# Steps 0 and 1 of a gated attention with an FFN behind it: one batch with 256 tokens a unit in place of two batches with 128

## The chip, the core and the metric

The kernel runs on one core of a Trainium2 chip. The metric is the device time of one execution in microseconds (us). The kernel before took 195.69 us, the median of three runs (195.66 to 196.28).

## What is computed

A recurrent attention with a decay for each key channel is followed by a feed-forward network with a ReLU gate. There are 4 batches, 8 heads, 768 tokens and 48 channels a head; the model width is 384 and the hidden width 1536.

```python
f = 1.0 / (1.0 + np.exp(-f_logit))
state = zeros((B, H, D, D)); y = zeros_like(q)
for t in range(S):
    state = f[:, :, t, :, None] * state + einsum('bhd,bhe->bhde', k[:, :, t], v[:, :, t])
    y[:, :, t] = einsum('bhd,bhde->bhe', q[:, :, t], state)
x = y.transpose(0, 2, 1, 3).reshape(B * S, H * D)          # 3072 x 384
out = (maximum(x @ w_gate, 0.0) * (x @ w_val)) @ w_out     # 1536 hidden
```

Inputs and output are float32 in HBM; the matmuls take bfloat16.

## The kernel before, in words

**Tiling.** The 768 tokens are cut into six steps of 128 tokens (`c` = 0 to 5). A step takes the four batches, two by two (pair `pr` = 0, 1). A step's attention gives 4 x 128 columns of `xT` (channels on partitions), and its FFN (`ffn_hidden`, `ffn_out`) works on these 512 columns: 12 blocks `j` of 128 hidden channels, each a gate group and a value group of three matmuls (L834), a ReLU on ACT (L840), a product on DVE (L844), then `w_out` (L877). In steps 0 to 2 the first six blocks run on 256 columns at a time (`halves`), so that a pair's FFN can begin before the other pair is done.

**Attention of a step.** ACT forms exp and log of the gate's logits (`f_in`, then `bneg`). TensorE sums the logs over tokens with a triangle of ones ("cum", L572 and L658). ACT takes exp of the sum with both signs. The products with `k` and `q` are the "hats" (POOL and DVE), which are transposed so that channels lie on partitions (`qkT`). TensorE multiplies them ("scores", L724), DVE masks the scores with a triangle (`ptm`, L734, four instructions a pair), and TensorE multiplies these with `vpad` and the query with the old state ("intra", L759). A product of `k` hats and `vpad` ("state", L810) updates the state on DVE and POOL (L543, L547, L549).

**Variants by step.** Step 0 is the only member of `twos`: a partition holds two neighbouring tokens of one of the pair's two batches, so a load of f, k or q has rows of 384 bytes in place of 192, and `v` is loaded one token a partition. `attention_pair` handles the pair's two batches as one. For the state update, `attention_back` transposes step 0's `k` back (L631) once the step's intra matmuls are done. In steps 1 and 2 (`pe_hats`) TensorE transposes the hats, eight 128x128 transposes a batch (L694), and DVE copies them out of PSUM (L699); in steps 3 to 5 a DMA transpose through the crossbar, issued from SP (L702), does this. In steps 0 to 2 intra is "tiled": 32-column array tiles give `xT`'s layout at once. In steps 3 to 5 it is "natural" (L767, L771), and a crossbar DMA transposes x (L795).

**Order.** A planner (`Plan`) is given every operation with a cost, a priority and the buffers that it touches, and lists each engine's instructions in one fixed order. Engines run in that order and wait on semaphores. Loads are issued from SP in a fixed order (`first`); the weights are issued from POOL. In `first`, `wg0@f0.1` means that weight slice 0 waits until the load of `f`, step 0, pair 1 has landed; `f1.0@wv1` likewise. While TensorE waits at the start, it runs matmuls on zeros (L938).

Of the kernel before, what the change touches and what calls it, by code (L numbers as in the profile page):

```python
# [299 lines left out]
def bass_hgrn2_outer__then__ffn_reglu_kernel(  # L300
# [10 lines left out]
    twos = (0,)  # L311
    pe_hats = {(1, 0), (1, 1), (2, 0), (2, 1)}
    halves = {0: 6, 1: 6, 2: 6}
    x_way = {(c, pr): "tiled" if c < 3 else "xbar" for c in range(6) for pr in range(2)}
    s_twin = {(c, pr) for c in range(6) for pr in range(2)} - {(0, 0), (1, 0)}
    y_twin = {(1, 1), (2, 0), (2, 1)}
# [5 lines left out]
    C = 128  # L322
# [30 lines left out]
    dec = [sb(f"dec{i}", [128, B, NP, 2], F32) for i in range(NA)]  # L353
# [20 lines left out]
    pick2 = sb("pick2", [128, 2], BF16)  # L374
    ident = sb("ident", [128, 128], BF16)
# [4 lines left out]
    pl = Plan({"bc": 2, "bc4": 4, "tp": 2, "s": 4, "y": 2, "kv": 1, "f": 4})  # L380
# [28 lines left out]
    def triangle(t, name, base, prio):  # L409
# [9 lines left out]
                                         pattern=[[0, 64], [1, 2]], channel_multiplier=-1), ["pick"], ["pick"], occ=0.3, prio=-20)  # L419
# [10 lines left out]
    add("DVE", lambda: ve.tensor_copy(pick2[:], same.ap[:, 0:2]), [same], ["pick2"], occ=0.1, prio=-19)  # L430
# [8 lines left out]
    for i in range(NA):  # L439
        fill("DVE", f"dec{i}", dec[i][:], 0.0, 32, -14)  # L440
# [20 lines left out]
    def load(n, c, b0, b1, after=()):  # L461
        last = tails.get("load")
        t = ld[n]
        both = c in twos and n != "v"
        if both:
            src = bass.AP(tensor=srcs[n].tensor, offset=b0 * H * S * D + c * C * D,
                          ap=[[2 * D, C // 2], [S * D, 2 * H], [1, 2 * D]])
            dst = bass.AP(tensor=t, offset=slot_of(n, c, b0 // 2) * 2 * HD, ap=[[NL[n] * 2 * HD, 128], [2 * D, H], [1, 2 * D]])
        else:
            src = bass.AP(tensor=srcs[n].tensor, offset=b0 * H * S * D + c * C * D,  # L470
                          ap=[[D, C], [S * D, (b1 - b0) * H], [1, D]])
            dst = t[:, slot_of(n, c, b0 // 2), :, :, :].rearrange("p b h d -> p (b h) d")
        op = add("SP", lambda: sy.dma_start(dst, src), [], in_keys(n, c, b0, b1),  # L473
                 occ=0.7 if both else 1.0, lat=0.9, prio=c * 100, after=after,
                 follows=[last] if last else [])
        tails["load"] = op
        dma(op, f"{n}{slot_of(n, c, b0 // 2)}", 0.95 * (b1 - b0), (64, 19, 27) if both else (128, 13.5, 23))
        return op
# [20 lines left out]
    loads, done = [], {}  # L499
    for item in first:  # L500
        item, _, behind = item.partition("@")
        gate = [done[behind]] if behind else []
        if item[0] == "w":
            op = load_w(item[:2], int(item[2:]), gate)
        else:
            c, pr = (int(x) for x in item[1:].split("."))
            op = load(item[0], c, 2 * pr, 2 * pr + 2, gate)
        done[item] = op
        if item[0] != "w":
            loads.append(op)  # L510

    def chain(line, *args, **kw):

        last = tails.get(line)
        tails[line] = add(*args, follows=[last] if last else [], **kw)
        return tails[line]
# [10 lines left out]
    def tokens(c, b, x, p, lo=0, hi=128):  # L527
        qi = (c * B + b) % NQ
        if c not in twos:
            return qkT[lo:hi, qi, x, p, :]  # L530
        row, two = NQ * 2 * NP * C, b % 2
        return bass.AP(tensor=qkT, offset=lo * row + (qi - two) * 2 * NP * C + x * 2 * NP * C + p * 2 * C + two,
                       ap=[[row, hi - lo], [2, C]])
# [18 lines left out]
    def attention_pair(c, b0):  # L552
# [3 lines left out]
        raw = {n: ld[n][:, slot_of(n, c, pr), :, :, :].rearrange("p b h d -> p (b h d)") for n in "fkq"}  # L556
        by_i = {n: raw[n].rearrange("p (h i d) -> p i h d", h=H, i=2) for n in "fkq"}
        key = {n: in_keys(n, c, b0, b0 + 2) for n in "fkq"}
        bi, e0, q0, ai = (w0 // 2) % NB, w0 % NE, w0 % NQ, c % NA
# [5 lines left out]
            follows=tails.pop("first q", []), **act_t(2 * HD))  # L565
        heads = lambda b_: b_.ap[:, 0:HD].rearrange("p (h d) -> p h d", h=H)
        for i in range(2):
            bc, ek = Bank("bc4"), Bank("bc4")

            def cum(i=i, bc=bc):  # L570
                for o in range(2):
# [3 lines left out]
            ex = expo[:, e0 + i, 0, :]  # L575
            add("ACT", lambda bc=bc, ek=ek: sc.activation(ek.ap[:, 0:HD], bc.ap[:, 0:HD], AF.Exp, scale=1.0),
                [bc], [ek], prio=P + 2 + i, opens=[ek], **act_t(HD))
            eqk = bc if i else f"expq{e0}_0"
            add("ACT", lambda bc=bc, i=i, ex=ex: sc.activation(bc.ap[:, 0:HD] if i else ex, bc.ap[:, 0:HD], AF.Exp, scale=-1.0),
                [bc], [eqk], prio=P + 2 + i, **act_t(HD))  # L580
            e, hi = ("DVE" if i else "POOL"), his[i]
            hk_op = add("DVE", lambda i=i, hi=hi, ek=ek: ve.tensor_tensor(hats[:, hi, 1, :, 0:D], by_i["k"][:, i], heads(ek), ALU.mult),
                        key["k"] + [ek, f"hats{hi}"], hk_(hi), prio=P + 2 + i, **dve_t(HD))
            add(e, lambda e=e, i=i, hi=hi, bc=bc, ex=ex: engine[e].tensor_tensor(
                hats[:, hi, 0, :, 0:D], by_i["q"][:, i], heads(bc) if i else ex.rearrange("p (h d) -> p h d", h=H), ALU.mult),
                key["q"] + [eqk, f"hats{hi}"], hq_(hi), prio=P + 3 + i, follows=[hk_op] if i else [], **elem_t(e, HD))
# [9 lines left out]
        for j in range(2):  # L596
            lo = 64 * j
            add("ACT", lambda lo=lo, j=j: sc.activation(
                dec[ai][lo:lo + 64, b0:b0 + 2, :, j].rearrange("p b n -> p n b"),
                tot.ap[lo:lo + 64, 0:2 * NP].rearrange("p (n b) -> p n b", n=NP), AF.Exp, scale=-1.0),  # L600
                [tot, f"dec{ai}"], [f"dec{ai}_{b}{j}{hh}" for b in (b0, b0 + 1) for hh in range(2)], prio=P + 10, **act_t(8))
        for x in (1, 0):
            tp = Bank("tp")

            def transposes(x=x, tp=tp):
                t16 = tp.ap[:, :].bitcast(BF16)
                for p in range(NP):
                    for i in range(2):
                        mm = te.transpose(t16[:, 2 * C * p:2 * C * (p + 1)].rearrange("q (r i b) -> q r i b", i=2, b=2)[:, :, i, :],
# [5 lines left out]
            e = "DVE" if x else "ACT"  # L615
            op = add(e, (lambda tp=tp, dst=dst: sc.activation(dst, tp.ap[:, :].bitcast(BF16), AF.Copy)) if e == "ACT"  # L616
# [3 lines left out]
            if not x and b0 == 0:  # L620
                tails["first q"] = [op]

    def attention_back(c, b, behind):
        w = c * B + b
        hi, qi = w % NH, w % NQ
        tp = Bank("tp")

        def transposes():
            t16 = tp.ap[:, :].bitcast(BF16)
            for p in range(NP):  # L630
                mm = te.transpose(t16[:, p * C:(p + 1) * C], tokens(c, b, 1, p), ident[:])  # L631
            return mm
        P = w * 10
        tails["transposes"] = add("PE", transposes, ["ident", f"qkT{qi}_10", f"qkT{qi}_11"], [tp], occ=0.3, lat=PE_L, prio=P + 30,
                                  opens=[tp], follows=[behind, tails["transposes"]])
        add("DVE", lambda: ve.tensor_copy(hats[:, hi, 1, :, :].rearrange("p h d -> p (h d)"), tp.ap[:, :].bitcast(BF16)[:, 0:4 * C]),
            [tp], hk_(hi), prio=P + 31, follows=[behind], **dve_t(256))

    def attention_front(c, b):
# [32 lines left out]
        if c < NC - 1:  # L672
            for j in range(2):
# [9 lines left out]
        add("POOL", lambda: gp.tensor_tensor(hq, qin[:, b % 2, :, :], ex[:, 0, :].rearrange("p (h d) -> p h d", h=H),  # L683
                                             ALU.mult),
            in_keys("q", c, b, b + 1) + [f"expq{ei // 2 * 2}_{ei % 2}", f"hats{hi}"], hq_(hi), prio=P + 2, **pool_t(HD))
# [21 lines left out]
    def attention(c, bs):  # L707
        units = []
        for b in bs:
# [5 lines left out]
                in_keys("v", c, b, b + 1) + [f"vpad{w % NV}"], [f"v_{w % NV}"], prio=w * 10 + (55 if c in twos else 3), **pool_c(HD))  # L715
# [58 lines left out]
        xi, ybank, yop = c % NX, {}, {}  # L774
        tiled = x_way[c, bs[0] // 2] == "tiled"
        for part in ([units] if tiled and (c, bs[0] // 2) in y_twin else [[u] for u in units]):
# [4 lines left out]
            op = chain("intra", "PE", rows, [t for u in part for t in need(u) + ([f"vpad{u[1] % NV}"] if tiled else [])], ys,  # L781
                       occ=(0.34 if c else 0.19) * len(part) + 0.235 if tiled else 0.38, lat=PE_L, prio=part[0][1] * 10 + 7, opens=ys)
            for u, y in zip(part, ys):
                ybank[u[0]], yop[u[0]] = y, op
        for b, w, _ in units:
# [12 lines left out]
            if c in twos:  # L798
                behind.append(yop[b])
                later.append(lambda b=b, w=w: update(c, b, w))  # L800
            elif c < NC - 1:
                update(c, b, w)

    def update(c, b, w):
# [9 lines left out]
        if c in twos:  # L814
            attention_back(c, b, behind[-1])
        chain("state", "PE", state, hk_(hi) + [f"hats{hi}", f"v_{w % NV}"], [kv],
              occ=0.18, lat=PE_L, prio=P + (32 if c in twos else 6), opens=[kv])
        new_state(kv, c, b, w, P + (25 if c in twos else 0))
# [50 lines left out]
    def ffn_out(g, bs, cuts=1):  # L869
# [14 lines left out]
        for b in bs:  # L884
# [4 lines left out]
            at = (b * S + g * C) * DM  # L889
            both = [(bass.AP(tensor=out.tensor, offset=at, ap=[[DM, C], [1, DM]]), osb[oi][:, :])]  # L890
# [4 lines left out]
    groups = {c: [(0, 2, range(0, n)), (2, 4, range(0, n)), (0, 4, range(n, NJ))] for c, n in halves.items()}  # L895
    pend = []
    for c in range(NC):
# [4 lines left out]
        behind, later = [], []  # L902
        for b in range(0, B, 2):
# [5 lines left out]
            attention(c, (b, b + 1))  # L909
        for rest in later:  # L910
            rest()
# [22 lines left out]
    order = pl.settle([(bk, warm_until if bk is spare else 0.0) for bk in banks], rounds=8, early=set(done.values()))  # L934
# [94 lines left out]
```

## Time and profile before

| What | Value |
|---|---|
| median of three runs | 195.69 us |
| profiled execution, its own time | 195.26 us |
| its span, first to last instruction | 193.5 us |
| TensorE matmul busy | 184.2 us (95%) |
| VectorE (DVE) busy | 106.1 us (55%) |
| ScalarE (ACT) busy | 111.0 us (57%) |
| GpSimd (POOL) busy | 75.9 us (39%) |
| DMA queue 1 (SP), share of 16 engines | 68.1% |
| granted TensorE clock | 1.00 |

The profiled execution is 0.43 us under the median. The span leaves 1.76 us around the instructions. PE is TensorE's matmul side and PEld its weight load. "Busy" of PE counts each matmul from its start to the end of its pipeline; several are in flight at once, so the distance of two starts, and not the mean length of one, is what a matmul costs in a run. A group line of the profile gives the line of code, engine, operation, tiles (out<-in), shape and count, then busy us and the mean ns of one, then the idle time of the engine just before them with what ended it.

### The profile page before, as it was taken

How to read it: one execution, taken by the hardware profiler on the slowest of the kernel's cores; microseconds unless marked ns; L12 is line 12 of the kernel's file. 1: busy time of each engine (PE TensorE's matmuls, PEld its weight loads, DVE VectorE, ACT ScalarE, POOL GpSimd, SP SyncE). 2: the span in 40 equal slices, each digit the busy share in tenths (PEclk: the TensorE clock that was granted, in tenths of full speed). 3: DMA queues.
4: the chain of work that ended last, by engine and by line, in shares of the span. 5: the costliest groups of instructions: out<-in, count | busy, mean ns of one | idle time of the engine just before them, and what ended most of it. 6: DMA issues, size and time to landing. Idle time of an engine off the chain costs nothing.

```text
span 193.5 us, 4448 instructions
## 1 busy us (share of the span) xinstructions
PE 184.2 (95%) x1773; PEld 110.7 (57%) x1790; DVE 106.1 (55%) x195; ACT 111.0 (57%) x250; POOL 75.9 (39%) x108
## 2 busy tenths in 40 slices
PE   6986898999999999999999999999999999999995
PEld 1445694465788556767755544554555555544564
DVE  7756884671668878354776643743635622443300
ACT  3777439763596779838757758377343544244322
POOL 8377002958275949783533471634230000000000
PEclk9999999999999999999999999999999999999999
DMA  4999999999898999999796998998954220111113
GB/s 131 276 283 207 206 201 207 207 199 239 199 244 167 202 201 192 231 193 247 161 192 132 194 207 172 221 226 170 204 87 106 64 61 0 41 41 44 41 43 119
DMA packets 118196, 31.74 MB, mean 164 GB/s; under 512 B 111136, under 2 KB 118176, under 8 KB 118176
## 3 DMA queue, kind: packets, MB, share of 16 engines
q1 hardware_dynamic: 114192, 27.93, 68.1%
q0 software_dynamic: 3984, 3.54, 11.4%
q8 instruction: 14, 0.23, 0.5%
q14 instruction: 6, 0.05, 0.1%
HBM read 25.95 MB, written 4.72 MB: 158 GB/s over the span
## 4 chain that ended last, share of the span: by engine, by line
PE 70%; DMA 16%; SPq 5%; ACT 2%; DVE 2%; POOL 2%; issue 1%
PE ps L834 36%; PE ps L877 23%; DMA q_in<-in_q_dram 6%; DMA wv<-in_moe_w_val_dram 5%; SPq L473 4%; DMA f_in<-in_f_logit_dram 3%; DMA v_in<-in_v_dram 3%; PE ps L724 2%; PE ps L658 2%; PE ps L694 2%; PE ps L759 1%; PE ps L810 1%; DVE ptm L734 1%; PE ps L857 1%; POOL hats L683 1%
## 5 line engine op out<-in xcount | busy, mean ns | idle before, releaser
L844 DVE TENSOR_TENSOR gT<-relu,ps 128x512 bf16<-128x512 bf16 (+1 forms) x90 | 51.2, 578 | 53.9 <-PE ps L834 38.8
L834 PE MATMUL ps<-xT,wv 128*128 128x512 bf16 (+1 forms) x263 | 60.2, 336 | 1.8 <-DMA wv<-in_moe_w_val_dram 1.3
L840 ACT ACTIVATE relu<-ps 128x512 bf16<-128x512 f32 (+1 forms) x90 | 45.3, 511 | 27.6 <-PE ps L834 27.0
L834 PE MATMUL ps<-xT,wg 128*128 128x512 bf16 (+1 forms) x261 | 59.6, 335 | 0.9 <-ACT relu L840 0.5
L877 PE MATMUL ps<-wo,gT 128*128 128x384 bf16 x276 | 49.5, 326 | 0.1
L877 PEld LDWEIGHTS ps<-wo,gT 128*128 128x128 bf16 x276 | 25.9, 98 | 17.2
L834 PEld LDWEIGHTS ps<-xT,wv 128*128 128x128 bf16 x270 | 24.6, 98 | 19.4 <-DMA wv<-in_moe_w_val_dram 1.7
L834 PEld LDWEIGHTS ps<-xT,wg 128*128 128x128 bf16 x270 | 25.2, 98 | 17.9 <-ACT relu L840 0.4
L734 DVE TENSOR_TENSOR ptm<-ps,tri 128x512 bf16<-128x512 f32 x48 | 30.5, 684 | 8.3 <-PE ps L724 8.2
L680 POOL TENSOR_TENSOR hats<-k_in,expo 128x384 bf16<-128x384 f32 x20 | 19.8, 1000 | 20.8 <-ACT expo L668 11.0
L887 ACT ACTIVATE osb<-ps 128x384 f32<-128x384 f32 x23 | 11.2, 489 | 26.1 <-PE ps L877 26.1
L683 POOL TENSOR_TENSOR hats<-q_in,expo 128x384 bf16<-128x384 f32 x20 | 19.8, 1000 | 6.5 <-DMA q_in<-in_q_dram 6.5
L549 POOL TENSOR_TENSOR st<-ssum,dec 128x384 bf16<-128x384 f32 x16 | 13.3, 830 | 15.7 <-DVE ssum L547 15.5
L649 ACT ACTIVATE f_in<-f_in 128x768 f32<-128x768 f32 x10 | 8.4, 843 | 12.1 <-DMA f_in<-in_f_logit_dram 12.1
L714 POOL CAST vpad<-v_in 128x384 bf16<-128x384 f32 x24 | 11.7, 505 | 3.2 <-DMA v_in<-in_v_dram 3.2
L547 DVE TENSOR_TENSOR ssum<-ps,st 128x384 f32<-128x384 f32 x16 | 8.8, 552 | 4.9 <-PE ps L810 4.9
L668 ACT ACTIVATE expo<-ps 128x384 f32<-128x384 f32 x20 | 9.9, 493 | 0.5 <-PE ps L661 0.3
L670 ACT ACTIVATE expo<-ps 128x384 f32<-128x384 f32 x20 | 9.9, 496 | 0.0
L699 DVE COPY qkT<-ps 128x1024 bf16<-128x1024 bf16 x8 | 5.5, 690 | 7.5 <-PE ps L694 7.4
L724 PEld LDWEIGHTS ps<-qkT 48*128 48x128 bf16 x192 | 5.4, 94 | 5.3 <-issue 1.9
L651 ACT ACTIVATE bneg<-f_in 128x768 bf16<-128x768 f32 x10 | 8.4, 836 | 0.0
L724 PE MATMUL ps<-qkT 48*128 48x128 bf16 x192 | 7.6, 217 | 0.6 <-ACT qkT L616 0.5
(76 smaller groups left out, 146.2 us busy)
## 6 DMA issues: line engine op xcount, KB each, us to landing
f_in<-in_f_logit_dram SPq DMA_DIRECT2D x12, 384.0 KB, 5.6
k_in<-in_k_dram SPq DMA_DIRECT2D x12, 384.0 KB, 4.9
q_in<-in_q_dram SPq DMA_DIRECT2D x12, 384.0 KB, 5.7
v_in<-in_v_dram SPq DMA_DIRECT2D x12, 384.0 KB, 5.3
out_dram<-osb SPq DMA_DIRECT2D x23, 192.0 KB, 2.4
wg<-in_moe_w_gate_dram POOLq DMA_DIRECT2D x3, 384.0 KB, 7.7
wv<-in_moe_w_val_dram POOLq DMA_DIRECT2D x3, 384.0 KB, 8.8
wo<-in_moe_w_out_dram POOLq DMA_DIRECT2D x3, 384.0 KB, 6.2
```

The lines of the kernel that those rows point to most:

```text
L549: add("POOL", lambda: gp.tensor_tensor(t4(s_new), t4(tmp), rate, ALU.mult), [key] + dk, [f"S{b}_{c % 2}"], prio=P + 8, **pool_t(HD))
L668: add("ACT", lambda: sc.activation(ex[:, 1, :], bc.ap[:, 0:HD], AF.Exp, scale=1.0), [bc], [f"expk{ei}"], prio=P + 1, **act_t(HD))
L680: add("POOL", lambda: gp.tensor_tensor(hk, kin[:, b % 2, :, :], ex[:, 1, :].rearrange("p (h d) -> p h d", h=H), ALU.mult), in_keys("k", c, ...
L683: add("POOL", lambda: gp.tensor_tensor(hq, qin[:, b % 2, :, :], ex[:, 0, :].rearrange("p (h d) -> p h d", h=H), ALU.mult), in_keys("q", c, ...
L714: add("POOL", lambda vin=vin, vout=vout: gp.tensor_copy(vout, vin.rearrange("p (n j) d -> p n j d", j=2)), in_keys("v", c, b, b + 1) + [f" ...
L724: mm = te.matmul(s[j].ap[:, p * C:(p + 1) * C], tokens(c, b, 1, p, lo, lo + D), tokens(c, b, 0, p, lo, lo + D))
L734: add("DVE", lambda mi=mi, j=j, s=s: ve.tensor_tensor(ptm[mi][:, j, :, :], s.ap[:, :].rearrange("p (n t) -> p n t", n=NP), mask, ALU.mult) ...
L834: mm = te.matmul(bank.ap[:, 0:n], wt[:, kt, j * 128:(j + 1) * 128], xT[xi][:, kt, n0:n1], start=(kt == 0), stop=(kt == NK - 1))
L840: add("ACT", lambda: sc.activation(relu[ri][:, 0:n], gate.ap[:, 0:n], AF.Relu), [gate], [f"relu{ri}"], prio=P, **act_t(n))
L844: add("DVE", lambda: ve.tensor_tensor(gT[gi][:, j, n0:n1], relu[ri][:, 0:n], val.ap[:, 0:n], ALU.mult), [val, f"relu{ri}"], [f"gT{gi}_{j}_ ...
L877: mm = te.matmul(o[b].ap[:, 0:DM], gT[gi][:, j, b * C:(b + 1) * C], wo[:, j, :], start=(j == 0), stop=(j == NJ - 1))
L887: add("ACT", lambda b=b, oi=oi: sc.activation(osb[oi][:, :], o[b].ap[:, 0:DM], AF.Copy), [o[b]], [f"osb{oi}"], prio=P, **act_t(DM))
```

## The change

`twos` becomes `(0, 1)`, and the unit of these steps is one batch with 256 tokens: step 0 takes batches 0 and 1, step 1 batches 2 and 3, each with tokens 0 to 255. Partition p holds tokens 2p and 2p+1, so tokens 0 to 127 lie in partitions 0 to 63 and tokens 128 to 255 in the other 64. All loads of both steps, `v` too, then have rows of 384 bytes. The two blocks of 128 tokens are two 64-row array tiles for scores, state and intra; the second block's state follows the first's within the unit, and the query of the second block meets that state in 12 matmuls. `attention_back` is gone; `mask2` (made on POOL) replaces the triangle. Step 1's hats are made as step 0's, four of them on POOL and two on DVE for the first unit. In both steps the copies of `qkT` run on DVE. Step 2's hats are transposed by the crossbar (`pe_hats` is empty). Step 3's x is "tiled".

```diff
-    twos = (0,)
-    pe_hats = {(1, 0), (1, 1), (2, 0), (2, 1)}
+    twos = (0, 1)
+    pe_hats = set()
...
-    x_way = {(c, pr): "tiled" if c < 3 else "xbar" for c in range(6) for pr in range(2)}
-    s_twin = {(c, pr) for c in range(6) for pr in range(2)} - {(0, 0), (1, 0)}
-    y_twin = {(1, 1), (2, 0), (2, 1)}
+    x_way = {(c, pr): "tiled" if c < 4 else "xbar" for c in range(6) for pr in range(2)}
+    s_twin = {(c, pr) for c in range(6) for pr in range(2)}
+    y_twin = {(2, 0), (2, 1), (3, 0), (3, 1)}
+    on_dve = {(1, 0, 0, 0), (1, 0, 0, 1)}
...
-        both = c in twos and n != "v"
+        both, one = c in twos, b1 - b0 == 1
         if both:
-            src = bass.AP(tensor=srcs[n].tensor, offset=b0 * H * S * D + c * C * D,
-                          ap=[[2 * D, C // 2], [S * D, 2 * H], [1, 2 * D]])
+            src = bass.AP(tensor=srcs[n].tensor, offset=(2 * c + b0 // 2) * H * S * D, ap=[[2 * D, C], [S * D, H], [1, 2 * D]])
...
+            for i in its:
+                for p in range(NP):
+                    for j in range(2):
+                        for b in range(2):
+                            mm = te.matmul(s[i][j].ap[64 * b:64 * b + 64, p * C:(p + 1) * C],
+                                           tokens(c, b0 + b, 1, p, 64 * j, 64 * j + D, i), tokens(c, b0 + b, 0, p, 64 * j, 64 * j + D))
...
+            for p in range(NP):
+                for i in range(2):
+                    for b in range(2):
+                        mm = te.matmul(kv[b].ap[:, p * 96:(p + 1) * 96],
+                                       hats[64 * b:64 * b + 64, his[i], 1, 2 * p:2 * p + 2, :].rearrange("p h d -> p (h d)"),
+                                       bass.AP(tensor=vpad[vs[i]], offset=64 * b * VW + p * VSTEP, ap=[[VW, 64], [64, 2], [1, D]]),
+                                       start=(i == 0), stop=(i == 1), skip_group_check=True)
...
+            for i in range(2):
+                for at, (n, p, col, j) in enumerate(todo):
+                    lo = 32 * (n % 4)
+                    for b in range(2):
+                        mm = te.matmul(y[b].ap[lo:lo + 32, n // 4 * C:(n // 4 + 1) * C],
+                                       vpad[vs[i]][64 * b:64 * b + 64, col:col + 32], ptm[ms[i]][64 * b:64 * b + 64, j, p, :],
+                                       start=(i == 0 and at < 4), stop=(b == 0 and i == 1 and at >= 12), skip_group_check=True)
+            for n, (p, m) in enumerate(blocks):
+                lo = 32 * (n % 4)
+                mm = te.matmul(y[1].ap[lo:lo + 32, n // 4 * C:(n // 4 + 1) * C],
+                               st[bt][0][:, p * SSTEP + 32 * m:p * SSTEP + 32 * m + 32], tokens(c, b0 + 1, 0, p),
+                               start=False, stop=(n >= 8), skip_group_check=True)
```

In the new order, PE's list begins with the whole attention of unit 0 but its 64 + 12 intra matmuls, then unit 1's cum, unit 0's intra, unit 1's transposes and state, then the first FFN group. Unit 2's cum stands after the ninth of the twelve FFN groups of step 0's second half; on ACT, unit 2's exp of `f_in` stands after the first ReLU of that half. Step 2's first two state products stand among step 0's `w_out` matmuls: the first behind 40 of the 48.

## The prediction

> **What bounds the kernel now.** I read the busy table first, then the 40 slices, the PE groups, the chain of waits, and the timeline of PE around each stage.
>
> ```profile
> PE 184.2 (95%) x1773; PEld 110.7 (57%) x1790; DVE 106.1 (55%) x195; ACT 111.0 (57%) x250; POOL 75.9 (39%) x108
> PE   6986898999999999999999999999999999999995
> DMA  4999999999898999999796998998954220111113
> ```
>
> TensorE is over 90% busy in every slice from the eighth (34 us) to the last but one. So the time is the moment at which TensorE stops being starved plus all matmuls left. DMA is full until about 145 us, though, so the start is DMA's. The chain of waits shows where it changes hands:
>
> ```profile
> 13.82 8.80 DMA wv<-in_moe_w_val_dram
> 22.64 6.21 DMA f_in<-in_f_logit_dram
> 28.88 0.84 ACT f_in L649
> 30.27 0.60 PE ps L834 x2
> ```
>
> The second value slice lands at 22.62; the first gate load of step 1 is issued behind it (`f1.0@wv1`), lands at 28.85, and ACT and then PE wait for it. From step 1's cum at 30.78 on, PE idles little: the waits on v (0.40 us at 100.8, 0.17 at 113.8) are the largest that I find.
>
> ```profile
> 100.81 0.34 PE L810 MATMUL ps<-vpad,hats 128*128 128x96 bf16 x4 [0.40 <-POOL vpad L714]
> 113.79 0.34 PE L810 MATMUL ps<-vpad,hats 128*128 128x96 bf16 x4 [0.17 <-POOL vpad L714]
> ```
>
> **What a matmul costs.** Each run in PE's timeline ends with one pipeline of 0.17 to 0.22 us; the rest of its length, by the count less one, is the distance of two starts.
>
> ```profile
> 12.21 0.63 PE L724 MATMUL ps<-qkT 48*128 48x128 bf16 x16 [0.53 <-ACT qkT L616]
> 14.00 0.41 PE L759 MATMUL ps<-ptm,vpad 128*32 128x128 bf16 x16
> 35.32 0.62 PE L694 MATMUL ps<-ident,hats 128*128 128x128 bf16 x8
> 35.78 0.34 PE L810 MATMUL ps<-vpad,hats 128*128 128x96 bf16 x4
> ```
>
> Transposes: (0.62-0.22)/7 = 0.057 us. Scores in two row tiles: (0.63-0.22)/15 = 0.027, half. Intra in four column tiles: 0.19/15 = 0.013, a quarter (I use 0.0142 = 0.057/4). State: 0.042. A 256-column FFN group of three is 0.33 us, a 512-column one 0.65, a w_out matmul 0.163 (starts in the timeline). Where a run of tiles follows full-array matmuls or precedes them, starts are 0.09 to 0.10 us further apart than these sums, so a visit to a tiled run costs 0.19.
>
> [...] Two stretches of the DMA view, the first with 384-byte rows (9.5 to 12 us), the second with 192-byte rows (70 to 75)[...]:
>
> ```profile
> DMA packets 2155, 0.80 MB, mean 322 GB/s; under 512 B 2155, under 2 KB 2155, under 8 KB 2155
> ...
> DMA packets 6042, 1.17 MB, mean 234 GB/s; under 512 B 6041, under 2 KB 6041, under 8 KB 6041
> ```
>
> A load of 0.393 MB takes 1.22 us at the first rate and 1.68 at the second: 0.46 less for each of ten loads (v of step 0, all eight of step 1). [...]
>
> **The change part by part.**
>
> *Loads ahead of the weights.* Two v loads come before the second value slice: 22.62 - 0.92 = 21.7. f1.0 then takes 6.21 - 0.46 = 5.75 (the two weight slices queued with it are the same): 27.45. ACT needs exp 0.84, a ReLU 0.38 that stands between, and log 0.84, less overlaps: before it was 1.93 from start of exp to cum. So unit 2's cum starts at 29.4. Bounds 29.0 to 30.4: less sharing with the weights, or no gain on f1.0's own wait.
>
> *Is PE there by then?* Unit 0: hats as before, to 9.5; transposes to 10.1; two qkT copies on DVE (0.69 each, the q copy left ACT, where it had waited for another load) to 11.1; two state steps 1.1 to 12.2; masks 4 x 0.62 to 14.7 (before: 15.15); intra to 15.8; unit 1's transposes, state, transposes to 17.4 behind its DVE hats (three of 0.55 after 14.7) and POOL's. FFN starts at 17.4 (before 16.58, but then it waited to 18.12 for wv). Five groups, scores, masks 19.9 to 22.4, seven groups with wv1 at 21.7, intra 22.8 to 23.9, two xT copies on ACT (2 x 0.49): second half at 25.0. Nine groups of 0.33: 27.95. PE waits 1.4 us, so an error of that size in this paragraph costs nothing; beyond it, it costs in full. The POOL masks (`mask2`, three small ones) lie in POOL's idle time before 8 us. Weights 2 move behind a hats product and a state step on POOL (about 2 us): nothing, as slice 1 still transfers; if that cover goes, up to 1 us.
>
> *The balance at that point.* At 30.78 before, PE had done step 0's FFN through six blocks and one 512-column group. At 29.4 after, three 256 groups and that one are open: 0.98 + 0.65, so 31.03. That is 0.25 later, with step 0's four states done in both (the 16 back transposes L631 and their DVE copies are gone; their 0.9 us lay ahead of the f1.0 wait, so that gain is lost in it).
>
> *Step 1.* A pair before: cum and totals 0.54, 16 transposes 0.90, scores 0.44, intra 56 x 0.0137 = 0.77, state 8 x 0.042 = 0.34; 2.99. A unit after: cum 4 x 0.165 + totals 0.20 = 0.86, transposes 0.90, 32 scores at a quarter 0.45, 16 states at half 0.34, 64 intra at an eighth (0.0071) 0.45, 12 more 0.17; 3.17. Two units: +0.36. If 64x32 tiles ran only four at a time, +0.91; if state did not pair up, another +0.67; a gain below nothing has no mechanism here. I take the eighth, as halves and quarters are shown. Mode changes: three visits and one change inside, 0.66 a unit, 1.32, against six visits, 1.14: +0.18.
>
> *Step 2.* 32 transposes L694 leave PE: -1.79; four DVE copies of 0.69 leave DVE, which isn't the bound. Four crossbar transposes (3.3 us to landing) join SP's queue, behind loads and a store that waits for ACT. PE needs the first pair's scores at about 60, 7 us after its hats can be made; hidden. Step 3: four x transposes leave SP; tiled against natural 28 x 0.0142 against 0.37 a batch: +0.1, and two visits +0.38.
>
> *Later waits.* SP and DMA lose ten times 0.46; crossbar work of step 2 and 3 about cancels. The two v waits (0.57) should shrink: -0.4. I set +0.1 for new small ones.
>
> Sum: 0.25 + 0.36 + 0.18 - 1.79 + 0.48 - 0.4 + 0.1 = -0.82. Against the profiled 195.26 that is 194.4; against the median 195.69 it is 194.9. Shifts under 0.3% (0.6 us) can't be told from no change here.
>
> **The rivals.** *Given back on PE or at f1.0 (chance 0.25, 195.6):* the eight-way tiles run four-way (+0.91), or f1.0 lands a microsecond later, each of which alone takes the 0.82 to about nothing. For it: ACT really stands at f_in with ReLUs queued behind, and PE's next groups behind those. Against: the trace scales at two and at four.
>
> *Slower by a late v of step 2 (chance 0.20, 197.0):* PE's order puts step 2's first state product behind 40 of step 0's 48 w_out matmuls. From 29.4: FFN 0.98 + 12 x 0.65, w_out 6.5, two units 6.34, step 2's cum 0.53, modes 1.32; 52.9. POOL must copy vpad by then, after two hats of 1.0 us, and that v landed at 56.1 before, by the trace's landing events; less ten times 0.46, 51.5. From 52.3 on it decides: everything behind it on PE waits, microsecond for microsecond. If the wo slices, issued while step 1's loads run, eat half the saving (2.3 us), it costs 1.5, and the crossbar behind these loads some 0.6 more: 194.9 + 2.1 = 197.0.
>
> *More than summed (chance 0.10, 193.3):* f1.0 at its early bound (-0.4), all late waits gone, and the few missed starts of 0.2 us around ReLU hand-overs gone as well.
>
> **How the numbers follow.** The forecast itself has 0.45, 194.2 to 195.3. Nearly all of it, with the better case, lies below 195.1, and its edge above that is about made up by the next case's edge below: faster 0.55. Same 0.25. Slower 0.20. The range takes in half of each outer case: 193.5 to 196.8.
>
> **What would show it.** Right: second value slice near 21.7, f1.0 near 27.4, ACT idle before f_in, cum of unit 2 near 29.4; a unit's 64 intra matmuls with starts 0.007 apart; no PE idle of more than 0.5 us after that; L694's group gone. Wrong: starts of 0.014 there, PE waiting for vpad near 53 or for a crossbar landing near 60, FFN's second half starting after 26.4.

## The result and the profile after

The change makes the kernel 12.6% slower: 221.05 us median (218.99 to 224.05, four runs) against 195.68 us on the same chip, a ratio of 1.126, interval 1.117 to 1.135. The profiled execution took 221.54 us, with a span of 219.8 us. A ratio, here and below, leaves out executions more than 1.5% above the fastest of their kernel; where many are left out, the medians of all are given too.

One edit of the change did nearly all of it. It stands among the lines that the diff above leaves out, and the prediction doesn't mention it. Since a unit's partition t now holds tokens 2t and 2t+1, a store of steps 0 and 1 writes its 128 rows in the order of even and odd tokens:

```diff
-            both = [(bass.AP(tensor=out.tensor, offset=at, ap=[[DM, C], [1, DM]]), osb[oi][:, :])]
+            both = [(bass.AP(tensor=out.tensor, offset=at, ap=([[DM, 2], [2 * DM, 64]] if g in twos else [[DM, C]]) + [[1, DM]]),
+                     osb[oi][:, :])]
```

The first dimension of the store is 2 and no longer 128. Nearly all of the loss follows from that 2.

The page of the kernel after, busy table and three rows of the 40 slices:

```profile
PE 191.6 (87%) x2030; PEld 112.9 (51%) x2030; DVE 107.6 (49%) x191; ACT 109.0 (50%) x244; POOL 74.9 (34%) x109
PE   7979699699948469999456989999999999999995
PEclk9999999999995969999978899999999999999999
DMA  6999999997474499993488599979897021000013
```

Before, PE held 9 from the eighth slice on. Now it drops twice, in slices 12 to 15 (60 to 82 us) and 20 to 22 (104 to 121 us), and DMA drops to 3 or 4 in slices 11, 13, 14, 19 and 20, where they begin. So these holes don't begin because DMA is overloaded: they begin while most of it stands idle, and DMA is full again when the late loads are caught up.

The chain of waits of the kernel after (start, length, what), its four long DMA pieces from 50 us on:

```profile
59.49 6.91 DMA qkT<-hats
...
70.64 7.73 DMA v_in<-in_v_dram
...
103.44 7.78 DMA f_in<-in_f_logit_dram
...
117.70 7.77 DMA q_in<-in_q_dram
```

A crossbar transpose and three different loads, each 6.9 to 7.8 us from issue to landing. Before, a load took 4.9 to 5.7 us at the median and a transpose 3.3. What they share is seen on SP, which issues them. SP's timeline of the kernel after (start, length, instruction):

```profile
51.14 0.69 SPq L963 DMA_DIRECT2D out_dram<-osb  x1
51.88 0.42 SPq L483 DMA_DIRECT2D k_in<-in_k_dram  x1
53.56 5.31 SPq L778 DMA_TRANSPOSE qkT<-hats  x1
58.92 0.53 SPq L963 DMA_DIRECT2D out_dram<-osb  x1
59.49 3.56 SPq L778 DMA_TRANSPOSE qkT<-hats  x1
63.09 0.65 SPq L963 DMA_DIRECT2D out_dram<-osb  x1
63.78 1.47 SPq L483 DMA_DIRECT2D q_in<-in_q_dram  x1
65.30 5.29 SPq L963 DMA_DIRECT2D out_dram<-osb  x1
70.64 0.67 SPq L483 DMA_DIRECT2D v_in<-in_v_dram  x1
71.36 5.31 SPq L483 DMA_DIRECT2D f_in<-in_f_logit_dram  x1
```

The same place before, where two stores are followed by two loads:

```profile
46.44 1.21 SPq L891 DMA_DIRECT2D out_dram<-osb  x2
47.69 1.15 SPq L473 DMA_DIRECT2D k_in<-in_k_dram  x1
48.89 2.08 SPq L473 DMA_DIRECT2D q_in<-in_q_dram  x1
```

A store that stands behind none costs SP 0.5 to 0.7 us in both kernels. It is the first or second instruction behind it that stands for 3.6 to 5.3 us: a transpose, another store, a load. The first store has left SP by then (at 51.83 us), and its packets run from 52.4 to 57.9. The DMA view of 54 to 58.5 us of the kernel after:

```profile
DMA  9999998405001122221111111111111111111111
GB/s 215 241 278 271 278 213 157 72 10 43 17 15 31 56 72 70 72 72 41 41 55 55 55 55 41 41 55 55 55 55 55 41 41 55 36 31 34 34 31 34
DMA packets 1204, 0.36 MB, mean 79 GB/s; under 512 B 1108, under 2 KB 1204, under 8 KB 1204
```

From about 56 us nearly every digit is 1, between 10 and 19% of 16 engines, which fits two of them (12.5%). The packets of the stores say it more exactly. Where the store's 1536-byte packets run, their summed time divided by the stretch that they fill is the number in flight:

| kernel | first dimension of the store | packets in flight | 128 packets take |
|---|---|---|---|
| before | 128 | 6.1 to 15 where one store ran alone | 0.63 to 1.35 us |
| after | 2 | 2.0 to 2.1 in all eight stores | 4.5 to 5.6 us |

A packet takes 65 to 94 ns before and 65 to 78 after (median of a store); what differs is how many run at once. The eight stores of steps 0 and 1 take 39 us in all (sum of the eight stretches). For about 22 of these no more than four packets of any kind are in flight.

The load behind the first store shows why the work behind comes late. It is k of step 2's second pair, 2048 packets of 192 bytes, and most of them run around 54 us, where the view above begins with 213 to 278 GB/s. But 249 of them, close to two sixteenths (256), run only after the store's last packet, at 57.9 us. The load lands 7.5 us after its issue has ended; before, the same load took 4.9.

PE's timeline of the kernel after shows what comes of it (in brackets: idle time before, and what ended it):

```profile
62.33 0.49 PE L905 MATMUL ps<-xT,wv 128*128 128x256 bf16 x3
66.65 1.04 PE L800 MATMUL ps<-qkT 48*128 48x128 bf16 x16 [3.83 <-DMA qkT<-hats]
67.62 0.82 PE L905 MATMUL ps<-xT,wg 128*128 128x256 bf16 x3
...
78.98 0.50 PE L883 MATMUL ps<-vpad,hats 128*128 128x96 bf16 x4 [5.26 <-POOL vpad L790]
```

PE stops for the transposes of step 2, then for its v, later for f and a transpose of step 3. There is a second loss: the three matmuls at 62.33 took 0.49 us, three of the same shape at 67.62, after the idle time, 0.82. Starts are 0.21 us apart there instead of 0.109, until 71.7, and starts lie up to twice as far apart again after the waits that end at 78.98, 112.52 and 118.24; the granted clock is 0.50 from 65.0 to 71.7, 78.6 to 82.0, 112.8 to 116.1 and 119.6 to 122.9 us, and 1.00 between. After the first three waits, of 3.8, 5.3 and 4.5 us, the half rate lasts another 5.1, 3.0 and 3.6 us. The fourth, of 1.91 us, differs: starts keep their usual distance behind it until about 119.5, and only then double.

```profile
118.24 0.62 PE L800 MATMUL ps<-qkT 48*128 48x128 bf16 x16 [1.91 <-DMA qkT<-hats]
...
119.33 0.61 PE L905 MATMUL ps<-xT,wv 128*128 128x256 bf16 x3
119.74 0.84 PE L905 MATMUL ps<-xT,wg 128*128 128x256 bf16 x3
```

The sum closes. PE's waits, added up over the waits view, were 6.0 us before and are 25.5 after: 19.5. Slow starts cost about 7.3 (an estimate: the distances above the usual ones in those four stretches). Together 26.8, where the span grew by 26.3; so the rest of PE's time is about half a microsecond shorter than before.

### The profile page after: what moved, and what is told of

Same layout as the page of the kernel before. It is cut to its first block, busy times and chain, and to the rows that moved or that the text cites. A ratio compares the mean times of both kernels' runs of the same rounds, so it can differ in the third digit from the quotient of the medians.

```text
span 219.8 us, 4949 instructions
## 1 busy us (share of the span) xinstructions
PE 191.6 (87%) x2030; PEld 112.9 (51%) x2030; DVE 107.6 (49%) x191; ACT 109.0 (50%) x244; POOL 74.9 (34%) x109
## 4 chain that ended last, share of the span: by engine, by line
PE 61%; DMA 25%; SPq 8%; POOL 2%; ACT 2%; issue 1%; POOLq 0%
PE ps L905 31%; PE ps L948 20%; DMA q_in<-in_q_dram 11%; SPq L483 6%; DMA wv<-in_moe_w_val_dram 4%; DMA f_in<-in_f_logit_dram 4%; DMA v_in<-in_v_dram 4%; DMA qkT<-hats 3%; PE ps L800 2%; SPq L963 2%; PE ps L883 1%; PE ps L835 1%; PE ps L734 1%; PE ps L928 1%; POOL hats L605 1%
## 5 line engine op out<-in xcount | busy, mean ns | idle before, releaser
L905 PE MATMUL ps<-xT,wv 128*128 128x512 bf16 (+1 forms) x270 | 64.2, 349 | 4.9 <-ACT xT L864 4.5
L905 PE MATMUL ps<-xT,wg 128*128 128x512 bf16 (+1 forms) x270 | 65.2, 353 | 1.0 <-ACT xT L712 1.0
L905 PEld LDWEIGHTS ps<-xT,wv 128*128 128x128 bf16 x270 | 26.4, 101 | 25.5 <-ACT xT L864 4.8
L756 POOL TENSOR_TENSOR hats<-k_in,expo 128x384 bf16<-128x384 f32 x16 | 16.0, 998 | 34.2 <-ACT expo L744 21.8
L810 DVE TENSOR_TENSOR ptm<-ps,tri 128x512 bf16<-128x512 f32 x32 | 20.5, 684 | 11.9 <-PE ps L800 11.9
L760 POOL TENSOR_TENSOR hats<-q_in,expo 128x384 bf16<-128x384 f32 x16 | 15.9, 1002 | 13.3 <-DMA q_in<-in_q_dram 13.3
L790 POOL CAST vpad<-v_in 128x384 bf16<-128x384 f32 x16 | 7.9, 505 | 14.3 <-DMA v_in<-in_v_dram 14.3
L883 PE MATMUL ps<-vpad,hats 128*128 128x96 bf16 x48 | 4.4, 219 | 8.0 <-POOL vpad L790 7.9
L666 DVE TENSOR_TENSOR ptm<-ps,mask 128x512 bf16<-128x512 f32 x16 | 9.9, 683 | 0.7 <-PE ps L657 0.7
L744 ACT ACTIVATE expo<-ps 128x384 f32<-128x384 f32 x16 | 7.9, 492 | 2.9 <-PE ps L737 2.5
L883 PEld LDWEIGHTS ps<-vpad,hats 128*128 128x128 bf16 x48 | 3.0, 102 | 10.4 <-POOL vpad L790 9.5
```

Source lines behind the costliest of these rows:

```text
L666: add("DVE", lambda i=i, j=j, mask=mask: ve.tensor_tensor(ptm[ms[i]][:, j, :, :], s[i][j].ap[:, :].rearrange("p (n t) -> p n t", n=NP), ma ...
L756: add("POOL", lambda: gp.tensor_tensor(hk, kin[:, b % 2, :, :], ex[:, 1, :].rearrange("p (h d) -> p h d", h=H), ALU.mult), in_keys("k", c, ...
L760: add(e, lambda: engine[e].tensor_tensor(hq, qin[:, b % 2, :, :], ex[:, 0, :].rearrange("p (h d) -> p h d", h=H), ALU.mult), in_keys("q", ...
L810: add("DVE", lambda mi=mi, j=j, s=s: ve.tensor_tensor(ptm[mi][:, j, :, :], s.ap[:, :].rearrange("p (n t) -> p n t", n=NP), mask, ALU.mult) ...
L905: mm = te.matmul(bank.ap[:, 0:n], wt[:, kt, j * 128:(j + 1) * 128], xT[xi][:, kt, n0:n1], start=(kt == 0), stop=(kt == NK - 1))
```

## Experiments

Theory W: the store's first dimension sets how many DMA engines carry it, two for a store of 2 x 64 rows. The traces show how many packets are in flight (2.0 to 2.1 with 2, 6.1 to 15 with 128), not which engine takes one; so "engines" in this theory is an inference. Against it stood, in turn: the new order of work (O), the stores' place on SP's queue (S), and the crossbar for step 2 (X). Ratios are to the kernel before on the same chip, with a 95% interval. In experiments 1 to 5, but for the stores, every engine's list is the same as in the kernel edited; in 6 to 11 the planner lists the work anew, so there the order of work changes along with the edit.

**1. Cut each store in two.** Same rows to the same places, as two stores whose first dimension is 64. Every engine's list is the same.

```diff
-            both = [(bass.AP(tensor=out.tensor, offset=at, ap=([[DM, 2], [2 * DM, 64]] if g in twos else [[DM, C]]) + [[1, DM]]),
-                     osb[oi][:, :])]
+            if g in twos:
+                both = [(bass.AP(tensor=out.tensor, offset=at + i * DM, ap=[[2 * DM, 64], [1, DM]]), osb[oi][64 * i:64 * i + 64, :])
+                        for i in range(2)]
...
```

> The changed kernel with each of the eight stores of steps 0 and 1 cut into two of 64 rows (64x384 twice in place of 2x64x384); each engine's list and its waits stay the same. Theory W (width): a store whose slowest dimension is 2 runs on two of the 16 DMA engines, about 5 us each time, and all that is queued behind it on these two engines waits. Then the loss goes: 194 to 196 us, my sum gave 194.9, no PE wait over 1.5 us, granted clock 1.0. Theory O (order): SP works its list in order, and stores and crossbar transposes that wait for ACT and POOL hold the loads behind them. Then nothing changes: 219 to 222 us.

Measured: 199.09 us, ratio 1.0166 (1.0096 to 1.0236). Of the 12.6%, 10.9 are gone. The packets of the eight stores go 5 to 12 at a time, the 128 of a store in 1.0 to 2.1 us. SP's timeline of this kernel, the same place as above:

```profile
50.68 1.76 SPq L967 DMA_DIRECT2D out_dram<-osb  x2
52.49 0.59 SPq L483 DMA_DIRECT2D k_in<-in_k_dram  x1
53.12 2.56 SPq L778 DMA_TRANSPOSE qkT<-hats  x1
55.73 1.22 SPq L967 DMA_DIRECT2D out_dram<-osb  x2
56.99 1.35 SPq L778 DMA_TRANSPOSE qkT<-hats  x1
```

Twice the stores, and no instruction stands for 5 us. The order is that of the kernel after, so O can hold no more than the remaining 1.7% (2.4% at the interval's end).

**2. Only step 0's stores cut.** The same edit, for four of the eight stores.

> The changed kernel with the four stores of step 0 cut into two of 64 rows, the four of step 1 left as 2x64x384. Theory W: the losses between 55 and 85 us go, those between 97 and 126 us stay: 205 to 212 us. Theory O: 219 to 222 us.

Measured: 207.87 us, ratio 1.0651 (1.0552 to 1.0749): 0.0485 above experiment 1 where eight narrow stores stand 0.109 above. The cost goes with the number of narrow stores.

**3. The narrow stores in the kernel before.** Nothing of the change but the shape; the rows land in another order within each block of 128.

```diff
-... ap=[[DM, C], [1, DM]] ...
+... ap=([[DM, 2], [2 * DM, C // 2]] if g < 2 else [[DM, C]]) + [[1, DM]] ...
```

> The kernel before with the eight stores of steps 0 and 1 given the shape 2x64x384 that they have in the changed kernel; their rows land in another order within a block of 128, the rest is the same, and so is each engine's list. Theory W: each store takes about 5 us on two engines and delays the loads behind it as in the changed kernel: 208 to 222 us, with crossbar and load landings near 7 us. Theory O: no change of order, so 195 to 197 us.

Measured: 222.38 us, ratio 1.1394 (1.1289 to 1.1498). The shape alone makes the kernel before as slow as the changed one. Its slices show the same two holes, and the drops of the clock behind them:

```profile
PE   7869998889849499999593099999999999999995
PEclk9988999999966979999969569999999999999999
DMA  5999999994381999989447979599794311000012
```

**4. Four and sixteen.** The same edit with first dimensions 4 and 16 (`[[DM, 4], [4 * DM, C // 4]]`, `[[DM, 16], [16 * DM, C // 16]]`).

> The kernel before with the same eight stores in the shape 4x32x384 (rows in another order within a block of 128). Theory W: four engines, half the time a store (2.5 us), part of it behind other queued work: 197 to 206 us, between before and the shape with 2. Theory O: 195 to 197 us.

Measured: 210.46 us, ratio 1.0783 (1.0689 to 1.0877).

> The kernel before with the eight stores of steps 0 and 1 written as 16 x 8 x 384 (row stride 16, then 1), where the earlier two kernels had 2 x 64 x 384 (222.4 us) and 4 x 32 x 384 (210.5 us); rows land in another order in the output, the same rows in the same number of packets. It tells the length of the first dimension from the mere fact that a store has three dimensions and jumps about in memory. Theory W (the first dimension sets how many DMA engines carry the store; with 16 all carry it): no wait, 195.0 to 197.0. Rival A (any such pattern of addresses is slow): rows jump more often than in the 2 x 64 form, so 210 or more.

Measured: ratio 1.0021 (0.9997 to 1.0045), spread over 20 runs with a median of 197.76 against 197.52. Packets in flight and the time for the stores of steps 0 and 1, with the first dimension alone changed in the kernel before:

| first dimension | packets in flight | 128 packets alone | ratio |
|---|---|---|---|
| 2 | 2.0 to 2.1 | 4.4 to 5.5 us | 1.139 |
| 4 | 3.3 to 3.8 | 2.5 to 4.2 us | 1.078 |
| 16 | 5 to 15 | 0.7 to 2.3 us | 1.002 |
| 128 (before) | 12 to 15 | 0.7 to 0.9 us | 1 |

Sixteen jumps about in memory as two and four do and costs nothing measurable. So it is neither the third dimension nor the addresses. I had expected four to cost half as much as it did: at 2.5 us a store I took most for hidden. PE's waits show why not: with four, one wait for v is 6.6 us long, with two 8.5. In step 0 the kernel before issues two stores in a row, and with four in flight their 256 packets take 5.8 to 5.9 us, longer than one store with two in flight.

**5. Narrow where no load stands behind.** The shape of experiment 3, on the stores of steps 3 and 4.

> The kernel before with the shape 2x64x384 on the eight stores of steps 3 and 4 in place of steps 0 and 1 (their rows in another order within a block of 128). They are issued after the last loads. Theory W: nothing that PE needs is queued behind them, so a store of 5 us costs nothing but some issue time: 195 to 197.5 us. If a narrow store costs by itself (osb buffers held, SP's time), 200 us or more.

Measured: ratio 1.0043 (1.0017 to 1.0070). Eight narrow stores cost 0.4% here and 14% there. What stands behind them on SP are six transposes and no load. Two of these transposes land 6.6 and 5.3 us after their issue has ended, and PE waits 0.7 us for one. The price isn't the store's own time; it is what is queued behind it and how soon PE needs that.

**6. The narrow stores from ACT's queue.** Does the store hold SP's queue (W-ring), or the engines (W-engine)?

```diff
-add("SP", lambda both=both: [sy.dma_start(d, s_) for d, s_ in both], ...
+add("ACT" if g in twos else "SP", lambda both=both, q=sc if g in twos else sy: [q.dma_start(d, s_) for d, s_ in both], ...
```

> The changed kernel with its stores left in the shape 2x64x384 but issued from ACT's queue. Two forms of theory W. W-ring: [...] most of the loss goes: 197 to 205 us. W-engine: the two engines are simply full for 5 us a store, whoever issues it, and every load has a sixteenth on each of them: 212 to 222 us.

Measured: 216.63 us, ratio 1.1006 (1.0939 to 1.1073). Another queue, with the order that goes with it, saves a fifth of the loss. PE's waits of this kernel (total, times, longest):

```profile
PE ps L800 <- DMA qkT<-hats: 14.3, 2, 8.7
```

Loads and transposes from SP still land late, behind 512 store packets that went two at a time for 18.6 us (52.7 to 71.3). The k load of step 2's second pair lands 13.3 us after its issue has ended (7.5 in the changed kernel, 4.9 before). Their own queue holds no narrow store any more. So SP's queue is not what holds most of the loss. That it is the engines is an inference by elimination, on the side of W-engine, whose range (212 to 222 us) held.

**7. The wide stores from ACT's queue.** Experiments 1 and 6 together.

> The wide-store kernel with the stores of steps 0 and 1 issued from ACT's queue in place of SP's, so that no load stands behind a store that waits for ACT; the planner sets the order anew. Theory S: SP waits 38 us in all for ACT before stores, v of step 2's second pair stands behind them, and PE waits 1.6 us for it; without that 195 to 197 us. Theory X or P: no gain, 198.5 to 201 us, since ACT also loses some 0.6 us for each issue.

Measured: ratio 0.9954 (0.9921 to 0.9987); times 195.68 that is 194.8 us. This is the lowest ratio of the study. It is not a safe gain: the medians of all executions, 197.38 us against 197.23, show none. S fits the rest: in experiment 1 the v load of step 2's second pair was issued at 63.19, behind eight half stores that waited for ACT, and PE waited 1.5 us for it. Here that wait has gone, and so are 1.6 us of waiting for transposes; how much of this is the queue and how much the new order wasn't taken apart. What PE waits for now, in a profiled execution of 199.14 us:

```profile
PE ps L632 <- POOL hats L605: 3.6, 2, 2.7
PE ps L695 <- DVE ptm L666: 1.4, 1, 1.4
```

**8. ACT's queue in the kernel before.** The control: only the edit of experiment 6, though here too the planner lists the work anew.

> The kernel before, with only one edit: the stores of steps 0 and 1 are issued from ACT's queue and no longer from SP's. It is the control for the change with wide stores from ACT's queue, which came to 0.9954 of the time before. Theory S (SP's stores wait for ACT's results in front of later loads and transposes, which matters only in the order of the changed kernel): before's loads of step 2 are early enough, its stores are short, so the time stays within 0.3%: 195.1 to 196.3. Rival (the queue by itself is worth it, and the change's gain of 0.5% is nothing but that): as fast as the changed kernel with ACT's queue, 194.0 to 195.0; then the change itself gains nothing.

Measured: ratio 1.0072 (1.0035 to 1.0108). The queue is no gain by itself; in the old order it costs 0.7%. The intervals of 7 and 8 don't touch, and the medians of all executions differ by as much (1.001 and 1.008 times the kernel before). So with the stores on ACT's queue the change does gain on the kernel before; against the kernel before as it was, no gain is sure. I had expected no change here; why it costs I didn't follow up beyond the profile, which shows PE waiting 1.5 us for a transpose and 1.4 for step 3's xT, both from SP's queue.

**9. w_out's slices later.** From experiment 7. Its largest wait is for q of step 1's second pair, which lands at 41.77, 10.3 us after its issue has ended, with two slices of w_out issued at 30.57 and 31.38 in flight beside it.

```diff
-... v1.0 wo0@q1.0 wo1 wo2 f1.1 k1.1 q1.1 v1.1
+... v1.0 f1.1 k1.1 wo0@k1.1 wo1 wo2 q1.1 v1.1
```

> The changed kernel with each store of steps 0 and 1 in two wide halves from ACT's queue, and one further edit: in the first list of loads the three slices of w_out wait for k of step 1's second pair and stand behind it, where they waited for q of the first pair. In the version without this edit PE waits 2.9 us at 40.8 for hats of q of step 1's second pair, which lands while two w_out slices transfer. Theory B (these slices take the bandwidth from that q): PE's wait at 40 falls by 2 us or more, with the slow starts of about 1 us after it, and the time falls by 2 to 4 us, to a ratio of 0.975 to 0.988. Rival L (w_out is then late): its first matmuls, at about 45, wait for its slices as long as q did; ratio 0.992 to 1.01, and a wait for w_out instead of hats in PE's waits.

Measured: ratio 0.9970 (0.9934 to 1.0006), no gain. The profiled execution took 202.37 us where the median is 197.67, so what it shows need not hold for the faster ones. That q lands at 36.49 now, 5 us earlier, so Theory B has the cause of that wait right. But the slices then share with f of step 2, which lands at 46.80, and PE's timeline of this kernel has:

```profile
48.69 0.48 PE L734 MATMUL ps<-bneg,tri 128*128 128x384 bf16 x1 [4.68 <-ACT bneg L727]
```

Rival L had the number right and the place wrong: not w_out was late, but the load behind it. DMA shows 8 or 9 in nearly every slice from 5 to 44 us; in this trace a wait is moved and not removed.

**10. Step 2's hats on PE again.** From experiment 1.

```diff
-pe_hats = set()
+pe_hats = {(2, 0), (2, 1)}
```

> The wide-store kernel (199.1 us) with step 2's hats transposed on TensorE again and copied by DVE, as before, in place of four crossbar transposes on SP. What is left of the gap to my 194.9 us is 4.2 us. Theory X (crossbar in SP's list): these four transposes hold step 2's later loads and are what makes v land late at 67.8 us; then the kernel gets faster although PE has 32 transposes (1.8 us) more: 196 to 198 us. Theory P (PE sum): the crossbar was hidden and the 1.8 us come back: 200 to 201.5 us. Theory S (stores in SP's list hold the loads): close to P, 199.5 to 201 us.

Measured: 203.18 us, ratio 1.0330 (1.0279 to 1.0380), 1.6% above experiment 1. X falls: the crossbar is a gain of some 3 us.

**11. Step 3's x by crossbar again.** From experiment 7.

```diff
-... "tiled" if c < 4 else "xbar" ...
+... "tiled" if c < 3 else "xbar" ...
```

> The changed kernel with each store of steps 0 and 1 in two wide halves from ACT's queue, and step 3's x transposed by crossbar as in the kernel before, not written in column tiles. It prices the last part of the change alone. The forecast's sum: tiles cost 0.1 us of matmuls and 0.38 of mode changes on PE, and the crossbar was hidden, so 0.5 us less than with the tiles: a ratio lower by 0.002 (0.993 where the version with tiles has 0.9954). Rival (four more crossbar transposes on SP's queue, behind step 2's and step 3's loads, land late): PE waits for xT in step 3, and the time is 0.5 to 3 us longer, a ratio of 0.998 to 1.01.

Measured: 201.86 us, ratio 1.0235 (1.0164 to 1.0306), 2.8% above experiment 7. PE's timeline of this kernel:

```profile
108.42 0.34 PE L734 MATMUL ps<-bneg,tri 128*128 128x384 bf16 x1 [0.66 <-ACT bneg L727]
...
110.85 0.62 PE L800 MATMUL ps<-qkT 48*128 48x128 bf16 x16 [1.75 <-DMA qkT<-hats]
```

A transpose of step 3's x is issued on SP at 105.56 to 106.81, between two transposes of hats; the second of these is issued at 106.86 to 109.43 and lands at 110.80, when PE can go on; at 112.10 it waits 0.63 us more, for x itself. After these waits PE's starts are up to twice their usual distance apart from 112.6 to 116 us. So the tiles are worth about 5 us here (4.5 by the medians of all executions), where the forecast had them as a loss. The edit also lets the planner place work from step 3 on otherwise, so not every tenth of it is the queue's.

## Why the prediction was wrong

**The step that failed** is in the paragraph on step 2: "Four crossbar transposes (3.3 us to landing) join SP's queue, behind loads and a store that waits for ACT ... hidden", and under later waits "SP and DMA lose ten times 0.46; crossbar work of step 2 and 3 about cancels." Both take the stores as they were: 0.6 us on SP, 2.4 us to landing. The access pattern of the store was in the diff, and I priced no part of it. The row of before to start from was there: 128 packets in 0.7 us with some 14 in flight. With the two in flight of the trace after, that makes about 5 us a store (an estimate; 4.5 to 5.6 was measured), eight times, in front of transposes and loads that PE needs. The two itself is in no view of before: none of its stores has a short first dimension. The list of signs of being wrong did hold one of the waits, "a crossbar landing near 60": PE met it at 62.8 and waited 3.83 us.

Of the recorded rivals, the late v of step 2 ended on the right side, by another mechanism. Its v landed at 51.12 (51.5 predicted, deciding from 52.3), and PE met the product at 55.4 without a wait; w_out's place was no bottleneck. The late v was that of the second pair, at 78.37, behind the fourth store.

**What held**, point by point:

- Loads: the second value slice landed at 21.32 (21.7 predicted), f1.0 at 26.43 (27.45), at 27.36 in experiment 1. Both came a little early.
- PE there by then: FFN's second half started at 25.48 (25.0). PE's timeline of the kernel after:

```profile
25.48 0.50 PE L905 MATMUL ps<-xT,wg 128*128 128x256 bf16 x3 [0.98 <-ACT xT L712]
...
28.44 0.33 PE L589 MATMUL ps<-bneg,upto 128*128 128x384 bf16 x1
...
42.69 0.62 PE L632 MATMUL ps<-ident,hats 128*128 128x128 bf16 x8 [2.01 <-POOL hats L605]
```

Unit 2's cum comes at 28.44 (29.4), behind the ninth group without a wait, where 1.4 us were predicted. With the three groups and the 512-column one that are open (0.98 + 0.65), the balance at that point is 30.07 against 30.78 before: 0.7 us ahead, not 0.25 behind.

- But the same timeline shows 2.01 us of waiting for hats at 42.69, the q of experiment 9 (landed 40.56). This is the term I left out of step 1: I followed f1.0 past the weights and not its sister loads past w_out, which is issued earlier now, two slices back to back at 29.65 and 30.45. A slice took 6.2 us to land before and 8.8 after. It takes the 0.95 us back that the balance had gained, and more.
- Step 1's matmuls. The intra run of unit 3 in the kernel after:

```profile
52.99 0.74 PE L695 MATMUL ps<-ptm,vpad 64*32 64x128 bf16 x64
```

  Reckoned as in the prediction, starts are (0.74-0.22)/63 = 0.0083 us apart (0.0071 said, 0.0142 feared). The 64-row scores come to 0.0135 (a quarter, as said), the state to 0.0207 (half, as said). The mis-sized term is 128 x 0.0012 = 0.15 us.
- Step 2: the sign was right; 1.79 us were said and the runs give some 3 (experiment 10); what goes beyond PE's own transposes wasn't taken apart. "Hidden" was right once the stores are wide: the transposes land at 57.65 and 60.13 in experiment 1, and PE waits for neither.
- Step 3: +0.48 us was said, and it is about -5 (experiment 11). PE's cost was counted and the relief of SP's queue set against step 2's transposes as cancelling. A queue isn't a sum: those of step 2 stand where SP had room, those of step 3 in front of a transpose of hats that PE waits for.

That the change with wide stores from ACT's queue comes out at 194.8 by its ratio, the very number of the forecast, is no proof of its sum, and is luck in part: the term of step 3 is off by some 5 us, the waits beside w_out's slices, which the sum left out, go the other way (2.7 us in experiment 7, and slow starts of about 1.6 us behind them), and what makes up the rest wasn't taken apart.

## What to carry to other kernels

Read the first dimension of every DMA that a change touches, stores too, even where bytes, rows and packets stay the same: a layout that interleaves tokens in partitions turns a store of 128 rows into 2 x 64, and here 2.0 to 2.1 packets were in flight then in place of 6.1 to 15. Cut such a store along its first dimension (5 to 12 in flight in experiment 1). Price a DMA by what is queued behind it: the same eight stores cost 14% in front of loads and 0.4% behind the last of them; and follow every load past every other transfer that the change moves, not only the one that is late first.

## What the runs showed of the hardware that I had not expected

- Packets in flight follow the first dimension of the store closely: 2.0 to 2.1 at 2, 3.3 to 3.8 at 4, up to 15 at 16 and at 128.
- Of the load behind a narrow store, an eighth of the packets (249 of 2048) ran only after the store's last one; the rest passed it.
- A narrow store from ACT's queue delays transposes and loads of SP's queue nearly as much as one from SP's own (1.101 against 1.126).
- A narrow store leaves SP in 0.5 to 0.7 us, and in three of the four cases shown the next DMA in 0.4 to 1.5; the one after that stands for 5.3.
- Tiles of 64x32, eight of them, ran with starts 0.0083 us apart, 1.17 times an eighth of 0.057.
- PE's starts fell to half rate about 1.3 us after a wait of 1.91 us had ended (the kernel after), and after waits of 1.75 and 0.63 us close together (experiment 11).
